# Six chunks of q, k and v requested at the start, decode steps spaced differently, and two memory layouts exchanged

## The chip, the cores and the metric

The kernel runs on one core of a Trainium2 chip. The metric is the device time of one execution in microseconds (us), as the median of several runs. The core has five engines with a queue of instructions each: TensorE (PE, matrix products), VectorE (DVE), ScalarE (ACT), GpSimd (POOL) and SyncE (SP). An engine works through its own queue in order: an instruction that waits holds up everything behind it on that engine. SP does nothing but issue transfers (through hardware descriptors, queue q1); POOL computes and also issues transfers (through software descriptors, queue q0).

## What is computed

Three stages, in fp32 accuracy: a decayed linear attention over 4 batches, 8 heads, 768 positions and 64 values a head; a gated product without a nonlinearity; and an FFN with a sigmoid-gated activation.

```
state = gamma * state + k[t]^T v[t];  y[t] = q[t] @ state / sqrt(64)     # x: 3072 x 512
h = (x @ w1) * (x @ w2) @ w3;  x = h @ w_out                             # 512 -> 1024 -> 512
h = x @ w_in;  out = (h * sigmoid(1.702 h)) @ w_out2                     # 512 -> 2048 -> 512
```

The weights arrive as 64-bit words and are turned into fp32 on the chip.

## The kernel before, in words

**Products.** Every fp32 operand of a large product is split into a rounded high part and a low remainder, and `mm3` (lines 240 to 242) issues three matmuls in place of one: high by high, weights high by operand low, weights low by operand high. The high part is made by a cast (`nc.scalar.copy` on ACT, in `split` or `upper`), the low part by a subtraction on DVE (`residue` or `lower`). So PE's second or third matmul of a group waits for DVE.

**Decoding weights.** `weight_steps` is a generator over 36 weight tiles (8 of w1 and w2, 4 of w_out, 8 of w3, 16 of the FFN). Each `yield` ends one step, which is one DVE instruction; a tile takes ten: two clamps (L184), two shifts (L192), two merges of the low word (L196), two sign merges (L205), and two subtractions for the low part (L137), which stand behind the clamps of the next tile. `magnitude` (L128) is the ACT instruction at the head of a tile; it reads `raw`, the buffer that a transfer on SP fills (`fetch`, L118). `work(n)` runs n steps, and so decides where in each engine's queue they stand.

**Attention (0 to about 155 us).** 24 chunks `c` of 128 tokens. For a chunk PE computes scores `s` (L339), the state update `u` (L365) and the output `y` (L389, L399); DVE masks the scores (`pt`, L351) and scales the output (`xb`, L411); ACT scales v (`vs`, L332) and copies the state. `load(c)` brings q, k, v of one chunk (1 MB) on POOL's queue into one of four buffers. `fill(c, at)` is called at four places `at` of a chunk and calls `work` there. From chunk 4 on, at the end of every second chunk, a gate follows (`first_gate`): 24 matmuls into `psg` with one decoded tile `wh`, `wl`; DVE multiplies its result into `h` (L279). Two chunks and a gate are called a period below.

**Mixed stage (155 to 417 us).** PE forms the gates of the other five blocks of 512 tokens and the product of w3 and w_out. POOL forms further operands (`st`, L159; `g`, L985 and L986) and stores them in DRAM (`sp`, `sw`, `sm`, `hd`). The last part takes its memory from pool `b2`.

**Blend (417 to 553 us).** A seven-product scheme for 2x2 blocks: 21 turns, `n` from 0 to 20, of 24 matmuls into `m`. In `blend`, turn n needs operand `l` (1 MB, loaded by SP from `hd`, L767, by `load_turn`), its cast `h` (ACT) and its remainder (DVE, L162). `todo(n)`, which is `ahead(n)`, does the remaining decode steps.

**FFN (553 to 1027 us).** `Expand` takes 4 blocks of 768 tokens by 8 weight tiles `left[j]`, in groups of 42 matmuls (`quad`) into banks `a`, `e`, `c`; a weight tile lies in one of eight slots (`slot`, table `SLOT`), is loaded from `sp` (`fetch_left`, L511) and split (`split_left`). `contract` is the last product, in 21 turns.

**Memory.** The pools of one stage lie on the addresses of the stage before. `reuse_waits="tile"` makes a new tile wait for the last user of each older tile that it overlaps, so the layout decides what a transfer waits for. In `b2` the tiles lie, in KiB from its start: `st` 0 to 8, `b12` 8 to 12, an unused gap 12 to 16, `g` 16 to 26 and 26 to 36. In the blend, on the same addresses, the operands `l` of turns 2, 3, 4 and 5 lie at 0 to 8, 24 to 32, 16 to 24 and 8 to 16.

Of the kernel before, what the change touches and what calls it, by code (L numbers as in the profile page):

```python
# [16 lines left out]
P = 128  # L17
NT = B * S
NCK = S // P
NC = B * NCK  # L20
# [22 lines left out]
def tile_kernel(  # L43
# [59 lines left out]

    fetched = used = 0
    allowed = R_BUFS

# [70 lines left out]
    def weight_steps():  # L177

        nonlocal used
        for i in range(len(tiles)):  # L180
            if i == 0:
                magnitude(i)
            for x in wx[i]:
# [19 lines left out]
            for n, (x, raw) in enumerate(zip(wx[i], raws[i])):  # L203
                bits = x.bitcast(I32)
                nc.vector.scalar_tensor_tensor(  # L205
                    bits, raw[:, :, 1], -(2**31), bits, ALU.bitwise_and, ALU.bitwise_or
                )
                if i < WI:
                    upper(i, n)
                used += 1  # L210
                fetch()
                fetch()
                magnitude(i + 1)
                if i >= WI and n:
                    seven(i, *wx[i])
                yield i + (i >= WI and n)
            if i < WI:
                lows[:] = [lambda i=i, n=n: lower(i, n) for n in range(2)]

    steps = weight_steps()  # L220
# [75 lines left out]
    class Attention:  # L296
# [21 lines left out]
        def load(self, c):  # L318
            t = self.tile("qkv", 2048, 4)
            for h in ((0, 1024), (1024, 2048)) if c == 0 else ((0, 2048),):  # L320
                nc.gpsimd.dma_start(t[:, slice(*h)], qkv[c][:, slice(*h)])
            qkt[c] = t[:, :1024].rearrange("p (a n t) -> p a n t", a=2, n=NP)
            kvt[c] = t[:, 1024:].rearrange("p (a h d) -> p a h d", a=2, h=H)

# [94 lines left out]
        def run(self, fill):  # L419

            self.scores(0)
            self.masked(0)
            for c in range(NC):
                if c + 1 < NC:
                    self.scores(c + 1)
                fill(c, 0)
                if c + 1 < NC:
                    self.masked(c + 1)
                fill(c, 1)
                self.updates(c)  # L430
                self.next_state(c)
                if c + 2 in range(2, NCK):
                    self.factors(c + 2)
                fill(c, 2)
                self.outputs(c)
                if c + 4 < NC:
                    self.load(c + 4)
                fill(c, 3)
# [59 lines left out]

    SLOT = "e", 0, 1, 2, 3, 4, 5, 6
    pools = {True: spare}  # L500
# [11 lines left out]

    def split_left(n):
        hi, lo = (left[n][:, w].rearrange("p b c -> p (b c)") for w in range(2))
        split(hi, lo, lo.bitcast(F32))

# [3 lines left out]
    class Expand:  # L520
# [75 lines left out]
        def run(self):  # L596
            self.open = nxt = None
            for n in range(1, NQ):
                left_tile(n)
                if n < NQ - 1:  # L600
                    fetch_left(n, nc.sync)
            self.results = [self.result(j) for j in range(2)]
            split_left(1)
            for s in range(NS):

                for j in range(NQ):

                    def step(at):
                        nonlocal nxt
                        more = s + 1 < NS  # L610
                        if more and (j, at) == (2, 3):
                            nxt = operands(s + 1, self.py)
                            next(nxt)
                        elif more and (j, at) in NEXT:
                            next(nxt)
# [7 lines left out]
            for _ in self.fourth():  # L623
                pass

    NEXT = (4, 3), (5, 1), (5, 3), (6, 3), (7, 0), (7, 2), (7, 3)
    RIGHT = dict(P1=0, P2=1, P3=2, P5=3, P6=4, P7=5, P4=6)
# [253 lines left out]
    with tc.manual_schedule():  # L881
# [4 lines left out]
        with (  # L886
            tc.tile_pool(name="p0", bufs=1, reuse_waits="tile") as p0,
            tc.tile_pool(name="ps0", bufs=1, space=PSUM, reuse_waits="tile") as ps0,
        ):
            attention = Attention(p0, ps0)  # L890
            nc.sync.dma_start(attention.dv, cv)
            nc.sync.dma_start(attention.mask, cmask)
            for c in range(4):
                attention.load(c)
# [14 lines left out]
            def fill(c, at):  # L909
                if (c, at) in ((0, 0), (1, 0)):  # L910
                    for _ in range(3 if c else 2):
                        fetch(held=True)
                if c > 1:
                    work(1 + (c > CPB and at == 2))
                while late:
# [14 lines left out]
        with (  # L930
# [43 lines left out]
            def gate_second(t, i, ab):  # L974
                nonlocal b12, g
                b = hb[0]
                if t % 2 == 0:
                    b12 = first_b.pop() if first_b else b12_tile()
                    g = pb.tile([P, 5, TB], F32, tag="g", bufs=2, name="g")
                    gate_out(b12, ab)  # L980
# [8 lines left out]

            g = None  # L990
            def b12_tile():
                return pb.tile([P, TB], F32, tag="b", bufs=2, name="b12")

            b12 = None
            for n, i in list(enumerate(ORDER))[1:]:
                nxt = ORDER[n + 1] if n + 1 < NB else None
                for t in range(KF):
# [16 lines left out]
                    while rows < KF and (complete > W3 + rows or (n, t) == (2, KF - 1)):  # L1014
# [4 lines left out]
                        if rows == KF:  # L1019
                            stage.close()  # L1020
                            pb = homes["st"] = stage.enter_context(
                                tc.tile_pool(name="b2", bufs=1, reuse_waits="tile")
                            )
                            st_ready = [pb.tile([P, 1024], F32, tag="st", bufs=2, name="st")]
                            first_b = [b12_tile()]
                            pb.tile([P, 1024], F32, name="gap")
        inner.close()
# [5 lines left out]
        def ahead(n):  # L1033
            nonlocal py, early
            if n == len(blends) - 2:
                split_left(0)
            if complete < len(tiles):
                work(4)
            elif n < 9:
# [125 lines left out]
```

## Time and profile before

| what | value |
|---|---|
| median of 3 runs | 1028.37 us (1027.59 to 1029.99) |
| the profiled execution | 1028.83 us; its span, from first to last instruction, 1027.1 us |
| busy share of the span: PE, DVE, ACT, POOL | 95%, 70%, 44%, 21% |
| mean granted clock of TensorE | 0.984 of full speed |
| moved by DMA | 268.73 MB, 262 GB/s on average |

The profile has one row for each instruction, with its start, its duration and the idle time of its engine ahead of it, with what ended that idle time in brackets. A busy share is an average over the stages; what a change is worth is read from the waits of the stage in which it acts. The granted clock has two levels here, 1.0 (2.4 GHz) and 0.5 (1.2 GHz); a value in between is a stretch with both.

### The profile page before, as it was taken

What the parts mean: (1) busy time and instruction counts of PE and PEld (TensorE: products, weight loads), DVE (VectorE), ACT (ScalarE), POOL (GpSimd) and SP (SyncE); (2) the same over time, 40 slices, a digit from 0 to 9 for tenths busy, and PEclk for the clock granted to TensorE, in tenths of its full rate; (3) what the DMA queues carried; (4) which work ended last, traced back from release to release, by engine and by line L of the source; (5) the groups of instructions that cost most, each with busy time, mean ns of one, the idle gap of its engine ahead of it and who ended that gap; (6) DMA issues with size and microseconds to landing.
All of it is one profiled execution on the core that took longest, in us unless ns stands there. A gap on an engine that the chain in (4) does not pass through costs nothing.

```text
span 1027.1 us, 14851 instructions
## 1 busy us (share of the span) xinstructions
PE 973.2 (95%) x5608; PEld 839.2 (82%) x5608; DVE 717.1 (70%) x959; ACT 449.7 (44%) x793; POOL 212.3 (21%) x248
## 2 busy tenths in 40 slices
PE   5899889999999999688998999999999999999998
PEld 5677768888888888567786999999999888888886
DVE  4766667888969867496774797685968555656662
ACT  4655564443322213263553664545455543445330
POOL 3010100048866745256202000000000000000000
PEclk9999999999999999889998999999999999999999
DMA  8778966568998979968956744646497978757871
GB/s 348 257 277 298 328 231 226 184 216 264 352 348 314 316 257 339 379 228 282 334 196 233 283 202 187 252 194 245 188 322 276 328 254 265 259 182 235 289 249 52
DMA packets 115032, 268.73 MB, mean 262 GB/s; under 512 B 7952, under 2 KB 69520, under 8 KB 105488
## 3 DMA queue, kind: packets, MB, share of 16 engines
q1 hardware_dynamic: 101264, 195.03, 54.2%
q0 software_dynamic: 13696, 72.75, 19.0%
q8 instruction: 44, 0.72, 0.3%
q14 instruction: 28, 0.23, 0.1%
HBM read 165.52 MB, written 102.24 MB: 261 GB/s over the span
## 4 chain that ended last, share of the span: by engine, by line
PE 48%; DMA 5%; POOL 4%; issue 3%; DVE 3%; ACT 1%; SPq 0%; POOLq 0%; DVEq 0%; ACTq 0%
PE m L241 9%; PE m L242 9%; PE m L240 9%; PE a L240 4%; PE a L242 4%; PE a L241 4%; PE e L242 2%; PE e L240 2%; PE e L241 2%; DMA hd<-g 2%; POOL st L159 1%; DMA raw<-in_wo_dram 1%; PE c L242 1%; PE c L240 1%; PE c L241 1%
## 5 line engine op out<-in xcount | busy, mean ns | idle before, releaser
L240 PE MATMUL psm<-xh,wh 128*128 128x512 f32 x320 | 124.6, 389 | 0.0
L242 PE MATMUL psm<-xh,wl 128*128 128x512 f32 x320 | 124.5, 389 | 0.0
L241 PE MATMUL psm<-xl,wh 128*128 128x512 f32 x320 | 124.5, 389 | 0.0
L240 PE MATMUL m<-h,op 128*128 128x512 f32 x320 | 124.5, 389 | 0.0
L242 PE MATMUL m<-h,op 128*128 128x512 f32 x320 | 124.5, 389 | 0.0
L241 PE MATMUL m<-l,op 128*128 128x512 f32 x304 | 118.3, 389 | 0.0
L662 ACT CAST h<-l 128x2048 fp32r<-128x2048 f32 x38 | 72.3, 1914 | 83.4 <-PE m L242 56.0
L663 DVE TENSOR_TENSOR l<-l,h 128x2048 fp32r<-128x2048 f32 x38 | 85.6, 2286 | 20.5 <-ACT h L662 20.5
L240 PE MATMUL a<-yh,op 128*128 128x384 f32 x256 | 86.2, 337 | 5.6 <-ACT s L531 5.1
L668 POOL DMA_DIRECT2D op<-sw x6 | 3.2, 531 | 400.5 <-PE a L242 220.1
L241 PE MATMUL a<-yl,op 128*128 128x384 f32 x256 | 85.9, 336 | 0.0
L242 PE MATMUL a<-yh,op 128*128 128x384 f32 x256 | 85.9, 336 | 0.0
L128 ACT ACTIVATE x<-raw 128x512 f32<-128x512 f32 x72 | 46.5, 675 | 75.2 <-DMA raw<-in_wo_dram 47.1
L240 PE MATMUL m<-h,wh 128*128 128x512 f32 x168 | 67.0, 399 | 9.5 <-ACT h L255 9.5
L240 PEld LDWEIGHTS psm<-xh,wh 128*128 128x128 f32 x320 | 60.1, 188 | 12.7 <-issue 0.2
L242 PEld LDWEIGHTS psm<-xh,wl 128*128 128x128 f32 x320 | 60.1, 188 | 12.5
L240 PEld LDWEIGHTS m<-h,op 128*128 128x128 f32 x320 | 60.1, 188 | 12.5
L242 PEld LDWEIGHTS m<-h,op 128*128 128x128 f32 x320 | 60.1, 188 | 12.3
L241 PEld LDWEIGHTS psm<-xl,wh 128*128 128x128 f32 x320 | 60.1, 188 | 12.3
L162 DVE TENSOR_TENSOR l<-l,h 128x2048 fp32r<-128x2048 f32 x19 | 46.4, 2441 | 33.2 <-ACT h L255 33.2
L242 PE MATMUL m<-h,wl 128*128 128x512 f32 x168 | 66.8, 398 | 0.0
L241 PEld LDWEIGHTS m<-l,op 128*128 128x128 f32 x304 | 57.1, 188 | 11.9
(149 smaller groups left out, 2228.2 us busy)
## 6 DMA issues: line engine op xcount, KB each, us to landing
gd<-g SPq DMA_DIRECT2D x32, 1344.0 KB, 4.7
qkv<-in_qkv_dram POOLq DMA_DIRECT2D x23, 1024.0 KB, 8.8
l<-gd SPq DMA_DIRECT2D x26, 768.0 KB, 6.7
l<-hd SPq DMA_DIRECT2D x19, 1024.0 KB, 6.9
raw<-in_w_dram SPq DMA_DIRECT2D x32, 512.0 KB, 5.5
hd<-g POOLq DMA_DIRECT2D x12, 1280.0 KB, 9.3
raw<-in_wo_dram SPq DMA_DIRECT2D x24, 512.0 KB, 8.3
l<-gd SPq DMA_DIRECT2D x24, 512.0 KB, 5.2
```

The source lines that it names most:

```text
L128: nc.scalar.activation(x, high, AF.Abs, scale=2.0**16)
L159: nc.gpsimd.tensor_tensor(out, x, y, op)
L162: nc.vector.tensor_tensor(lo, x, hi.bitcast(F32), ALU.subtract)
L240: nc.tensor.matmul(ps, wh, xh, start=start, stop=False, skip_group_check=True)
L241: nc.tensor.matmul(ps, wh, xl, start=False, stop=False, skip_group_check=True)
L242: nc.tensor.matmul(ps, wl, xh, start=False, stop=stop, skip_group_check=True)
L662: nc.scalar.copy(hi, x.bitcast(F32))
L663: nc.vector.tensor_tensor(x, x.bitcast(F32), hi.bitcast(F32), ALU.subtract)
L668: queue.dma_start(t.bitcast(F32), sw[PART[name]])
```

## The change

1. **Loads of q, k, v.** `load` is called for six chunks at the start instead of four. Chunks 4 and 5 take four buffers of the weight tiles (`wg`), which the last gate tiles need only later; the first half of chunk 0 is issued by SP ahead of its other transfers instead of by POOL. `load(c + 4)` starts at chunk 2. Three fetches of raw weights move from chunk 1 to chunk 2.
2. **Decode steps in the attention.** Tile 0's subtractions follow at once, and `fill` runs three steps more in chunks 4 and 5, so all later steps stand three places earlier.
3. **Pool `b2`.** The order of its tiles is `g` 0 to 10 and 10 to 20, `st` 20 to 28, `b12` 28 to 32 KiB.
4. **Decode steps in the blend.** `magnitude` is no longer issued right behind the fetch, but at the next call of `ahead`; and `ahead` runs two steps a turn instead of four up to turn 4.
5. **FFN.** The table `SLOT` gives tiles 1 to 7 the slots 1, 3, 4, 0, 2, 5, 6 instead of 0 to 6, and `left[1]` is cast by DVE instead of ACT. `NEXT0` moves two operand steps of the first block to later places.

```diff
@@ weight_steps
-            if i == 0:
-                magnitude(i)
+            magnitude(i)
...
-                magnitude(i + 1)
+                if not lazy:
+                    magnitude(i + 1)
...
+            if i == 0:
+                for k, f in enumerate(lows):
+                    f()
+                    yield k
+                lows.clear()
@@ Attention.load
-            t = self.tile("qkv", 2048, 4)
-            for h in ((0, 1024), (1024, 2048)) if c == 0 else ((0, 2048),):
-                nc.gpsimd.dma_start(t[:, slice(*h)], qkv[c][:, slice(*h)])
+            if c in (4, 5):
+                qk, kv = (
+                    homes["wg"].tile([P, 1024], F32, tag="wg", bufs=16, name=f"c{x}") for x in "qk"
+                )
+            else:
+                t = self.tile("qkv", 2048, 4)
+                qk, kv = t[:, :1024], t[:, 1024:]
+            if c in (0, 4, 5):
+                (nc.gpsimd if c else nc.sync).dma_start(qk, qkv[c][:, :1024])
+                nc.gpsimd.dma_start(kv, qkv[c][:, 1024:])
+            else:
+                nc.gpsimd.dma_start(t, qkv[c])
@@ Attention.run
-                if c + 4 < NC:
+                if 6 <= c + 4 < NC:
                     self.load(c + 4)
@@
-    SLOT = "e", 0, 1, 2, 3, 4, 5, 6
+    SLOT = "e", 1, 3, 4, 0, 2, 5, 6
@@ Expand.run
-            split_left(1)
+            split_left(1, nc.vector.tensor_copy)
...
+    NEXT0 = (4, 3), (6, 0), (6, 2), (6, 3), (7, 0), (7, 2), (7, 3)
@@
-            for c in range(4):
+            for c in range(1, 6):
                 attention.load(c)
@@ fill
-                if (c, at) in ((0, 0), (1, 0)):
+                if (c, at) in ((0, 0), (2, 0)):
                     for _ in range(3 if c else 2):
                         fetch(held=True)
                 if c > 1:
-                    work(1 + (c > CPB and at == 2))
+                    work(1 + (c >= CPB and at == 2) + (c in (CPB, CPB + 1) and at == 3))
@@ gate_second
-                    b12 = first_b.pop() if first_b else b12_tile()
-                    g = pb.tile([P, 5, TB], F32, tag="g", bufs=2, name="g")
+                    b12 = pb.tile([P, TB], F32, tag="b", bufs=2, name="b12")
+                    g = first_g.pop() if first_g else g_tile()
...
+                            first_g = [g_tile()]
                             st_ready = [pb.tile([P, 1024], F32, tag="st", bufs=2, name="st")]
-                            first_b = [b12_tile()]
-                            pb.tile([P, 1024], F32, name="gap")
@@ ahead
+            lazy = True
             if n == len(blends) - 2:
                 split_left(0)
             if complete < len(tiles):
-                work(4)
+                for i in sorted(raws):
+                    if i >= complete:
+                        magnitude(i)
+                work(2 if n < 5 else 4)
```

PE's instructions keep their order throughout. On DVE, in a period of the attention (from one gate's product `h` to the last row before the next one) the queue before reads:

```order
L279 TENSOR_TENSOR h<-h,psg 128x512
L351 TENSOR_TENSOR pt<-s,mask 128x512 x2
L192 TENSOR_SCALAR x<-x 128x512
L196 SCALAR_TENSOR_TENSOR x<-raw,x 128x512 x2
L411 TENSOR_TENSOR xb<-y,dy 128x512
L205 SCALAR_TENSOR_TENSOR x<-raw,x 128x512 x2
L351 TENSOR_TENSOR pt<-s,mask 128x512 x2
L184 TENSOR_SCALAR x<-x 128x512 x2
L137 TENSOR_TENSOR wl<-x,wh 128x512
L411 TENSOR_TENSOR xb<-y,dy 128x512
L137 TENSOR_TENSOR wl<-x,wh 128x512
L192 TENSOR_SCALAR x<-x 128x512
```

and after the change:

```order
L285 TENSOR_TENSOR h<-h,psg 128x512
L366 TENSOR_TENSOR pt<-s,mask 128x512 x2
L205 SCALAR_TENSOR_TENSOR x<-raw,x 128x512 x2
L184 TENSOR_SCALAR x<-x 128x512
L426 TENSOR_TENSOR xb<-y,dy 128x512
L184 TENSOR_SCALAR x<-x 128x512
L138 TENSOR_TENSOR wl<-x,wh 128x512
L366 TENSOR_TENSOR pt<-s,mask 128x512 x2
L138 TENSOR_TENSOR wl<-x,wh 128x512
L192 TENSOR_SCALAR x<-x 128x512 x2
L426 TENSOR_TENSOR xb<-y,dy 128x512
L196 SCALAR_TENSOR_TENSOR x<-raw,x 128x512 x2
```

The same twelve rows stand there; the two subtractions `wl`, which stood on either side of the period's last `xb`, now both stand ahead of it, the first one ahead of the second `pt`. On ACT, at the start of the blend, the queue before reads (casts `h` of turn 1 and of weights, then the rows of turns 0 and 1):

```order
L255 CAST wh<-wl 128x1024
L128 ACTIVATE x<-raw 128x512 x2
L821 COPY s<-m 128x512 x2
L255 CAST h<-l 128x2048
L255 CAST wh<-wl 128x1024
```

and after the change:

```order
L261 CAST wh<-wl 128x1024
L129 ACTIVATE x<-raw 128x512
L838 COPY s<-m 128x512 x2
L261 CAST h<-l 128x2048
L261 CAST wh<-wl 128x1024
```

One of the two reads of `raw` has left the place ahead of turn 2's cast `h`; it now stands behind turn 3's. On SP the loads around that place stand, before and then after:

```order
L767 DMA l<-hd_77 128x4x512 x2
L118 DMA raw<-in_wo_dram 128x1024
L767 DMA l<-hd_77 128x4x512
L118 DMA raw<-in_wo_dram 128x1024
L767 DMA l<-hd_77 128x4x512
```

```order
L784 DMA l<-hd_77 128x4x512 x3
L119 DMA raw<-in_wo_dram 128x1024
L784 DMA l<-hd_77 128x4x512
L119 DMA raw<-in_wo_dram 128x1024
L784 DMA l<-hd_77 128x4x512
```

The first `raw` moved behind a third load of `l`.

## Rows read from the trace of the kernel before

**Rows 1.** Waits of PE, whole span: total us, times, longest.

```profile
PE psg L242 <- DVE wl L137: 14.0, 8, 3.6
PE m L240 <- ACT h L255: 9.5, 1, 9.5
...
PE m L241 <- DVE l L162: 5.7, 4, 3.0
PE a L240 <- ACT s L531: 5.1, 1, 5.1
PE s L339 <- DVE pt L351: 2.8, 1, 2.8
```

**Rows 2.** Busy time by stretch: PE, PEld, DVE, ACT, POOL, PE clock, DMA share, GB/s.

```profile
24.53:30.00 5.47, 5.47 (x74) 4.83 (x76) 4.79 (x10) 3.62 (x12) 0.06 (x1) 0.69 0.84 346
54.95:68.51 13.56, 12.31 (x153) 9.78 (x152) 9.32 (x17) 7.38 (x23) 1.33 (x2) 1.00 0.84 300
133.00:139.81 6.81, 6.81 (x23) 5.18 (x23) 2.07 (x4) 1.86 (x7) 0.00 (x0) 0.75 0.68 259
438.65:445.50 6.85, 5.32 (x13) 3.86 (x14) 6.85 (x7) 5.75 (x7) 2.67 (x4) 0.54 0.58 226
...
560.31:567.00 6.69, 6.69 (x28) 6.69 (x29) 3.90 (x3) 2.88 (x4) 0.00 (x0) 0.69 1.02 425
```

**Rows 3.** Timeline of PE: a gate's first matmul; turn 2's first matmul.

```profile
61.31 0.50 PE L240 MATMUL psg<-xh,wh 128*128 128x512 f32 x1
...
438.65 0.80 PE L240 MATMUL m<-h,wh 128*128 128x512 f32 x1 [9.49 <-ACT h L255]
```

**Rows 4.** Timeline of DVE: start, duration, idle before.

```profile
22.14 1.74 DVE L184 TENSOR_SCALAR x<-x 128x512 f32<-128x512 f32 x1 [1.17 <-ACT x L128]
...
58.89 0.68 DVE L411 TENSOR_TENSOR xb<-y,dy 128x512 f32<-128x512 f32 x1
...
60.69 1.28 DVE L351 TENSOR_TENSOR pt<-s,mask 128x512 f32<-128x512 f32 x2
61.89 0.75 DVE L184 TENSOR_SCALAR x<-x 128x512 f32<-128x512 f32 x2
62.56 0.68 DVE L137 TENSOR_TENSOR wl<-x,wh 128x512 fp32r<-128x512 f32 x1
...
464.17 4.52 DVE L162 TENSOR_TENSOR l<-l,h 128x2048 fp32r<-128x2048 f32 x1
...
525.11 0.55 DVE L467 CAST yh<-yr 128x768 fp32r<-128x768 f32 x1
```

**Rows 5.** Timeline of POOL at the start: five loads of q, k, v.

```profile
1.28 2.76 POOL L321 DMA_DIRECT2D qkv<-in_qkv_dram  x5 [0.37 <-issue]
```

**Rows 6.** Timeline of SP at the start of the blend.

```profile
406.10 23.12 SPq L767 DMA_DIRECT2D l<-hd  x2
429.33 0.55 SPq L118 DMA_DIRECT2D raw<-in_wo_dram  x1
```

**Rows 7.** DMA issues in 60:150, 413:415, 428.6:429: count, KB, us to landing.

```profile
raw<-in_w_dram SPq DMA_DIRECT2D x7, 512.0 KB, 10.1
...
hd<-g POOLq DMA_DIRECT2D x1, 1280.0 KB, 8.8
...
l<-hd SPq DMA_DIRECT2D x1, 1024.0 KB, 5.2
```

**Rows 8.** Timeline of ACT: a blend's raw read, turn 18's copy, the FFN's cast.

```profile
435.18 0.66 ACT L128 ACTIVATE x<-raw 128x512 f32<-128x512 f32 x1 [15.17 <-DMA raw<-in_wo_dram]
...
542.23 0.59 ACT L821 COPY s<-m 128x512 f32<-128x512 f32 x1 [2.13 <-PE m L242]
...
558.20 1.68 ACT L255 CAST op<-op 128x1792 fp32r<-128x1792 f32 x1 [4.50 <-DMA op<-sp]
```

**Rows 9.** Timeline of POOL: the last two stores of `g`.

```profile
413.67 0.57 POOL L987 DMA_DIRECT2D hd<-g  x1 [0.30 <-POOL g L986]
...
421.59 0.57 POOL L987 DMA_DIRECT2D hd<-g  x1 [0.30 <-POOL g L986]
```

More of the change, by code (lines that the diff above doesn't have):

```diff
@@ L104, in tile_kernel @@
     fetched = used = 0
+    lazy = False
     allowed = R_BUFS
@@ L318, in load @@
         def load(self, c):
-            t = self.tile("qkv", 2048, 4)
-            for h in ((0, 1024), (1024, 2048)) if c == 0 else ((0, 2048),):
-                nc.gpsimd.dma_start(t[:, slice(*h)], qkv[c][:, slice(*h)])
-            qkt[c] = t[:, :1024].rearrange("p (a n t) -> p a n t", a=2, n=NP)
-            kvt[c] = t[:, 1024:].rearrange("p (a h d) -> p a h d", a=2, h=H)
+            if c in (4, 5):
[10 more added lines that the diff above has]
+                nc.gpsimd.dma_start(t, qkv[c])
+            qkt[c] = qk.rearrange("p (a n t) -> p a n t", a=2, n=NP)
+            kvt[c] = kv.rearrange("p (a h d) -> p a h d", a=2, h=H)
         def bank(self, kind):
@@ L511, in fetch_left, with split_left @@
         queue.dma_start(t.bitcast(F32), sp[n])
-    def split_left(n):
+    def split_left(n, copy=nc.scalar.copy):
         hi, lo = (left[n][:, w].rearrange("p b c -> p (b c)") for w in range(2))
-        split(hi, lo, lo.bitcast(F32))
+        copy(hi, lo.bitcast(F32))
+        residue(hi, lo, lo.bitcast(F32))
     def left_parts(n, name, k):
@@ L597, in run @@
             self.open = nxt = None
-            for n in range(1, NQ):
+            for n in sorted(range(1, NQ), key=lambda n: SLOT[n]):
                 left_tile(n)
-                if n < NQ - 1:
-                    fetch_left(n, nc.sync)
+            for n in range(1, NQ - 1):
+                fetch_left(n, nc.sync)
             self.results = [self.result(j) for j in range(2)]
-            split_left(1)
+            split_left(1, nc.vector.tensor_copy)
             for s in range(NS):
@@ L613, in step @@
                             next(nxt)
-                        elif more and (j, at) in NEXT:
+                        elif more and (j, at) in (NEXT if s else NEXT0):
                             next(nxt)
@@ L890, in tile_kernel @@
             attention = Attention(p0, ps0)
+            attention.load(0)
             nc.sync.dma_start(attention.dv, cv)
             nc.sync.dma_start(attention.mask, cmask)
-            for c in range(4):
+            for c in range(1, 6):
                 attention.load(c)
@@ L988, in gate_second, with g_tile @@
                 hb.pop(0)
[L990 to L994, printed above, removed]
+            def g_tile():
+                return pb.tile([P, 5, TB], F32, tag="g", bufs=2, name="g")
+            b12 = g = None
             for n, i in list(enumerate(ORDER))[1:]:
@@ L1033, in ahead @@
         def ahead(n):
-            nonlocal py, early
+            nonlocal py, early, lazy
+            lazy = True
             if n == len(blends) - 2:
```

## The prediction

> **What bounds the kernel now.** PE is busy 95% of the span, and its instructions keep their order and number; the change can only take away idle time of PE, and time in which PE runs at the lower clock. I read the waits of PE first [rows 1]: five of them hold 37 us, in three places. Eight gates of the attention wait 14.0 us for `wl`; one turn of the blend waits 9.5 us for a cast `h`, and four wait 5.7 us for a remainder `l`; the FFN's first group waits 5.1 us for a copy on ACT; chunk 2 waits 2.8 us for a mask. Then the busy time by stretch [rows 2]: behind the long waits PE is busy throughout, yet at a granted clock between 0.54 and 0.75, so each long wait costs a second time. Last the timelines, for what is late at each place.
>
> **The gates.** In a period DVE starts `xb` at 58.89 and, after two sign merges, the second mask at 60.69; the gate's first matmul runs at 61.31, but DVE comes to the first `wl` only at 62.56, behind mask and clamps [rows 3, 4]. That is the wait: on average (14.0 - 3.6) / 7 = 1.5 us, and 3.6 once. After the change three instructions of the same forms stand between the first mask and `xb` (two merges and a clamp instead of two merges and a shift), so `xb` keeps its place. Behind it stand one clamp (0.75 / 2 = 0.38) and the first `wl` (0.68): 58.89 + 0.68 + 0.38 + 0.68 = 60.6, ahead of the gate's start by 0.7. The mask (1.28) and the second `wl` (0.68) end at 62.6; the second half of the gate needs it from 64.2 on (the gate lasts 68.51 - 61.31 - 1.5 = 5.7). What now stands behind, two shifts and two merges, is wanted by nobody before the next period. The period shrinks from 13.56 to 12.06; DVE is busy 9.32 of it, ACT 7.38 [rows 2], so neither becomes the bound. I take all 14.0; at most 15.5, since PE's modelled matmul ends shorten the idle time that a row shows. The longest wait is followed by 6.81 us at clock 0.75 [rows 2]: (1 - 0.75) x 6.81 = 1.7 us, gone with it. Sum 15.7.
>
> **The start.** In chunk 2 a clamp on DVE takes 1.74 us instead of 0.38 [rows 4]; a multiplication by POOL runs at the same moment, because a load stands ahead of it in POOL's queue and waits for a buffer. After the change no load stands between the first four multiplications, so they are done earlier, and the mask behind the clamp comes 1.4 earlier: the wait of 2.8 halves. The 5.47 us behind it ran at 0.69 [rows 2], which is 1.7 us; the 1.4 us that stay are no longer than the gates' waits, beside which the clock stays at 1.00 (54.95 to 68.51 in [rows 2]), so I take all 1.7. Bounds for both: 0 (the raw weights are later now, and the wait stays) and 4.5. SP's first load takes one issue out of POOL's queue, 2.76 / 5 = 0.55 [rows 5]: I take 0.5, bounds 0 and 0.55. Sum 3.6.
>
> **The blend.** Now SP stands for 23 us at the load of turn 3's `l` [rows 6], whose memory (24 to 32 KiB) overlaps both buffers of `g`; the last store of `g` is issued at 421.59 [rows 9], and the load leaves about 428.7 (the row ends at 429.2, and one issue takes 0.55). The raw weights behind it are issued at 429.33 [rows 6], and ACT, which reads them ahead of turn 2's cast, stands 15.17 us until 435.18 [rows 8]. PE is free for turn 2 at 438.65 - 9.49 = 429.16 [rows 3]. After the change that read stands behind turn 3's cast. But turn 2's own load now overlaps the first buffer of `g` (0 to 10 KiB), so it waits for the store issued at 413.67, which landed 8.8 us later, at 422.5 [rows 7, 9]; before, it waited for none of these. That store shared the engines with turn 2's load, which is now behind it, so it lands somewhat sooner: 421 to 422.5, I take 421.5. A load of `l` takes 5.2 us alone and a transfer beside others 8.8 [rows 7]; the last store of `g` runs beside it, I take 6.5. Landing 428.0; the cast takes 1.9 (1.68 for 1792 columns [rows 8], so for 2048): 429.9, a wait of 0.7 instead of 9.5, so 8.8 gained; bounds 9.5 (landing 426) and 5.5 (landing 431.3, a wait of 4.0). With so short a wait the 5.32 busy us at clock 0.54 [rows 2] go too: 2.4 us, bounds 0 and 2.4. Turn 4's load now waits for the last `g` and lands about 434 to 437, while its turn starts at about 441: hidden, with 3 us of cover after the cast. The remainders: 5.7 us [rows 1], of which 3.0 where DVE needed 4.52 us for one beside POOL's work [rows 4]. DVE does two steps a turn less, some 1.3 us; but in turn 2 the remainder still follows the cast and PE waits about 2 for it, and POOL's work meets DVE at other turns. I leave 3.5 of the 5.7: 2.2 gained, bounds 0 and 3.5. Sum 13.4, bounds 5.5 and 15.4.
>
> **The FFN.** ACT stands 4.50 us until `left[1]` has landed and casts it for 1.68 [rows 8], with the first group's copies behind it. Slot 0, where it lay, overlaps by the sizes the weights of the blend's last turn; slot 1 overlaps those of turn 18 and earlier, and turn 18 ends at 542.2 [rows 8]. The load therefore starts two turns earlier and lands by 551 even at 8.8 us. Its cast is on DVE now: 0.55 for 768 columns [rows 4], an estimated 1.3 for 1792, and a remainder of 1792 / 512 x 0.68 = 2.4; done by 555, while the second group, which needs it, starts some 6 us after 553 (36 matmuls of 384 columns against 24 of 512 in 5.7). ACT goes on to the copies at once. The wait of 5.1 goes, and with it (1 - 0.69) x 6.69 = 2.1 at the lower clock [rows 1, 2]. Sum 7.2, bounds 2 (DVE late instead of ACT) and 7.2.
>
> **Sum.** 15.7 + 3.6 + 13.4 + 7.2 = 39.9. The mixed stage is not touched but for addresses; PE is busy there without a gap. From this I take off 0.9 for transfers that come late in the shorter attention: in a period DMA has a share of 0.84 and moves 300 GB/s x 13.56 us = 4.07 MB [rows 2]; in 12.06 us the share is 0.94, and in the two periods in which four reloads of 256 KB run, 1.06, that is up to 1.5 us too much in all. The Trainium skill ("DMA: Bandwidth & Descriptors", Specifications) puts a core's limit at HBM at about 358 GB/s; by it the reload periods need 12.8 us and 1.5 us are lost. The FFN's start moved 425 GB/s [rows 2], above that figure; at that rate nothing is lost. So 39.0: the profiled execution, 1028.83, becomes 989.8. It lies 0.5 above the median shown; as a median 989.4.
>
> **Rivals.** (a) DMA becomes the bound of the attention: raw weights or reloads come late in each period from chunk 13 on, and up to four gates wait 1.5 us again. For it the share of 0.94; against it that q, k, v are asked six chunks ahead. 1.5 to 6 us back: 991 to 996. (b) Turn 2's load is late: at the upper bounds the wait is 4.0, the clock falls again (1.5), the remainders gain nothing (2.2): 7 back, 996. For it that 1 MB now starts at 421.5 and not at 406.10 [rows 6]; against it that the raw weights no longer stand in the way. (c) `left[1]` is late and DVE stands for it: 5 back, 995. (d) The gates wait as before, because DVE reaches `xb` late and everything behind it with it: 14 back, 1003; against it DVE's idle 4.2 us in the period. (e) Slower than before: POOL's queue, which now always holds further loads, starves SP's raw weights, and ACT stands at their read ahead of the casts of each tile. They land 10.1 us after their issue [rows 7] and are asked two periods, 24 us, ahead; each us beyond that costs PE one per tile. To eat 39 us, eight tiles must lose 5 us each: it decides from a landing time of 29 us, three times the row; then 1029 or more. The Trainium skill (same page, Queues, rings and completion order) says that a DMA engine takes turns between the queues that have work for it; by that rule SP's loads get their turn however long POOL's list is. No row here has six loads asked ahead. (f) The waits only change their place, and the time stays within 0.2%.
>
> **Chances.** Forecast as summed 0.56 (985 to 993); (a) 0.12; (b) 0.16; (c) 0.05; (d) 0.04; two of these together, 996 to 1004, 0.02; (e) 0.03; (f) 0.02. So faster by more than 0.2% (what a measurement of this kernel can tell from no change) 0.95, within it 0.02, slower 0.03. The range runs from all upper bounds together (15.5 + 1.7, 5.05, 15.4, 7.2: 44.9, so 983) to 1001, which takes in (a), (b) and (c) and leaves out less than 2 in 10. The likeliest case's own range is 985 to 993.
>
> **What the profile will show.** Right: no wait of `psg` for `wl` above 0.3 us, and a period of about 12; a mean clock above 0.99; turn 2's cast no later than 1 us after PE is free for it; ACT's read of `raw` behind turn 3's cast, with no wait of PE behind it; `left[1]` loaded at the end of turn 18, and no idle PE at the FFN's start. Wrong: a wait of PE for q, k, v or of ACT for `raw` in the attention (a, e); `l` of turn 2 landing after 430 (b); a long remainder beside POOL's `st` in turns 5 to 7; DVE idle ahead of its cast of `left[1]` (c). It would be wrong as a whole if PE, freed of these waits, met a wait that they hid, for instance for `xb` in the attention.

## The result, and the profile after

The changed kernel takes 1011.59 us (median of 4 runs, 1010.01 to 1012.48) against 1028.78 of the kernel before on the same chip: a ratio of 0.9831, interval 0.9813 to 0.9849. It is faster, as forecast, but by 17 us where 39 were forecast, and it lies outside the range of 983 to 1001. Its profiled execution has a span of 1009.2 us at a mean granted clock of 0.986.

Where the 17.9 us between the two profiled executions (1028.83 and 1010.95) came from is seen in the starts of the stages on PE (the first matmul into `psg`, `psm`, `m` and `a` in its timeline). The forecasts of the start and the gates are given in one sum, with the 0.9 for late transfers taken off:

| stage | before | after | gained | forecast |
|---|---|---|---|---|
| up to the second gate | 47.32 | 50.88 | -3.6 | } 18.4 |
| second gate to the mixed stage | 108.1 | 92.8 | 15.3 | } |
| mixed stage | 261.3 | 261.3 | 0 | 0 |
| blend | 136.1 | 132.7 | 3.4 | 13.4 |
| first stage of the FFN | 241.0 | 238.4 | 2.6 | 7.2 |

PE's waits after, which answer to [rows 1]:

```profile
PE s L354 <- DMA qkv<-in_qkv_dram: 9.4, 3, 4.4
PE m L247 <- DVE l L163: 5.6, 4, 1.8
PE m L246 <- ACT h L261: 4.9, 2, 3.2
PE a L246 <- ACT s L547: 2.9, 1, 2.9
PE psg L246 <- ACT xh L261: 2.9, 1, 2.9
...
PE s L354 <- DVE pt L366: 1.7, 1, 1.7
...
PE psg L248 <- DVE wl L138: 0.4, 1, 0.4
```

The 14.0 us for `wl` are gone. The 9.5 us for one cast `h` are now 4.9 us for two; the 5.7 us for remainders are 5.6, at other turns; the 5.1 us for a copy at the FFN's start are 2.9; and 2.9 us for `xh` are new, ahead of the first gate. The first line, the waits of the first chunks for q, k and v, was 8.3 us before: the first load now comes 1.2 us earlier, but that of chunk 1 comes later, and PE starts chunk 1 0.75 us later than before (before, then after):

```profile
10.14 2.08 PE L339 MATMUL s<-qkv 64*128 64x128 f32 x16 [2.46 <-DMA qkv<-in_qkv_dram]
```

```profile
10.89 2.08 PE L354 MATMUL s<-qkv 64*128 64x128 f32 x16 [4.41 <-DMA qkv<-in_qkv_dram]
```

Busy time by stretch, with the columns of [rows 2]: the start, the first gate, a period, turn 2, turn 7, the FFN's start.

```profile
20.00:30.00 10.00, 8.29 (x128) 7.02 (x127) 6.96 (x17) 6.65 (x22) 2.14 (x4) 0.83 1.03 417
30.00:35.96 5.96, 2.40 (x50) 1.83 (x49) 1.30 (x4) 2.35 (x4) 0.08 (x1) 0.92 1.01 414
35.96:44.92 8.96, 8.55 (x25) 5.98 (x25) 6.22 (x12) 6.42 (x21) 0.00 (x0) 0.67 0.44 158
56.57:68.62 12.05, 12.05 (x154) 9.86 (x153) 9.32 (x17) 7.20 (x23) 1.67 (x2) 1.00 0.87 312
420.49:430.40 9.91, 8.17 (x25) 6.19 (x25) 9.00 (x8) 5.86 (x7) 0.84 (x1) 0.66 1.03 388
454.36:464.34 9.98, 8.16 (x24) 6.29 (x25) 7.89 (x9) 3.30 (x4) 3.69 (x7) 0.66 0.78 274
542.92:549.60 6.68, 6.68 (x29) 6.68 (x30) 2.77 (x3) 2.88 (x4) 0.00 (x0) 0.74 0.89 367
```

The period is 12.05 us, where 12.06 was forecast, and PE is busy all of it. But behind each new wait PE runs at a clock of 0.66 to 0.74, as behind the old ones: a turn that takes 5.44 us undisturbed takes 9.9. PE's rows at the new waits, and ACT's, which shows what was late:

```profile
35.96 0.79 PE L246 MATMUL psg<-xh,wh 128*128 128x512 f32 x1 [2.94 <-ACT xh L261]
...
420.49 0.64 PE L246 MATMUL m<-h,wh 128*128 128x512 f32 x1 [3.16 <-ACT h L261]
...
454.36 0.50 PE L246 MATMUL m<-h,wh 128*128 128x512 f32 x1 [1.73 <-ACT h L261]
...
542.92 0.45 PE L246 MATMUL a<-yh,op 128*128 128x384 f32 x1 [2.95 <-ACT s L547]
```

```profile
34.22 0.66 ACT L129 ACTIVATE x<-raw 128x512 f32<-128x512 f32 x1 [3.09 <-DMA raw<-in_w_dram]
...
418.54 1.90 ACT L261 CAST h<-l 128x2048 fp32r<-128x2048 f32 x1 [5.97 <-DMA l<-hd]
...
451.86 0.66 ACT L129 ACTIVATE x<-raw 128x512 f32<-128x512 f32 x1 [7.99 <-DMA raw<-in_wo_dram]
452.42 1.89 ACT L261 CAST h<-l 128x2048 fp32r<-128x2048 f32 x1
...
542.39 0.48 ACT L547 COPY s<-a 128x384 f32<-128x384 f32 x1 [3.90 <-DMA yd<-s]
```

All four are ACT standing for a transfer: a raw weight ahead of the cast `xh` that the first gate needs; the load of `l` of turn 2; a raw weight ahead of turn 7's cast; and, at the FFN, a *store*, since the first copy `s` lies where a buffer of the blend lay that is still being written to `yd`. How long these transfers took (the median where there are two), from the DMA issues of 21:22, 409.8:410.6, 441.5:442.3 and 534:538 (count, KB, us to landing):

```profile
raw<-in_w_dram SPq DMA_DIRECT2D x2, 512.0 KB, 10.8
...
l<-hd SPq DMA_DIRECT2D x1, 1024.0 KB, 8.5
...
raw<-in_wo_dram SPq DMA_DIRECT2D x1, 512.0 KB, 9.9
...
yd<-s POOLq DMA_DIRECT2D x2, 256.0 KB, 6.8
```

Of the two raws in the first line, the one that ACT stands for took 12.4 us. Between 20 and 36 us DMA moves 414 to 417 GB/s without a gap. That is again above the limit of about 358 GB/s that the Trainium skill ("DMA: Bandwidth & Descriptors", Specifications) gives for a core at HBM; here the trace decides.

### The profile page after: what moved, and what is told of

It reads as the page before. It is cut to its first block, busy times and chain, and to the rows that moved or that the text cites. A ratio compares the mean times of both kernels' runs of the same rounds, so it can differ in the third digit from the quotient of the medians.

```text
span 1009.2 us, 14859 instructions
## 1 busy us (share of the span) xinstructions
PE 973.4 (96%) x5608; PEld 840.3 (83%) x5608; DVE 716.2 (71%) x960; ACT 447.4 (44%) x792; POOL 205.2 (20%) x249
## 3 DMA queue, kind: packets, MB, share of 16 engines
q0 software_dynamic: 13840, 72.23, 18.4%
## 4 chain that ended last, share of the span: by engine, by line
PE 47%; DVE 2%; DMA 1%; issue 0%; ACT 0%; POOL 0%; DVEq 0%; ACTq 0%
PE m L247 9%; PE m L248 9%; PE m L246 9%; PE a L247 4%; PE a L246 4%; PE a L248 4%; PE e L248 2%; PE e L247 2%; PE e L246 2%; PE c L248 1%; PE c L247 1%; PE c L246 1%; DMA yd<-s 1%; DVE g L579 1%; DVE yl L483 0%
## 5 line engine op out<-in xcount | busy, mean ns | idle before, releaser
L680 DVE TENSOR_TENSOR l<-l,h 128x2048 fp32r<-128x2048 f32 x38 | 85.6, 2287 | 20.3 <-ACT h L679 20.3
L248 PEld LDWEIGHTS psm<-xh,wl 128*128 128x128 f32 x320 | 60.1, 188 | 12.4
L247 PE MATMUL m<-l,wh 128*128 128x512 f32 x152 | 61.7, 406 | 5.6 <-DVE l L163 5.6
```

The lines of the kernel that those rows point to most:

```text
L247: nc.tensor.matmul(ps, wh, xl, start=False, stop=False, skip_group_check=True)
L248: nc.tensor.matmul(ps, wl, xh, start=False, stop=stop, skip_group_check=True)
L680: nc.vector.tensor_tensor(x, x.bitcast(F32), hi.bitcast(F32), ALU.subtract)
```

## The experiments

All start from the changed kernel, and every one was timed beside the kernel before. Stage starts and lengths are read as in the table above; "turns 1 to 3" is the sum of three turns, 16.3 us undisturbed. A turn is measured from its first matmul to the next turn's, so a wait ahead of a turn's first matmul counts to the turn before. The times were taken in four sittings, one of them on another chip, in which the kernel before took 1028.8 to 1030.7 us; between sittings the ratios compare better than the medians.

| kernel | median us | ratio to before, interval | first gate | mixed stage | blend | FFN, first stage |
|---|---|---|---|---|---|---|
| changed | 1011.59 | 0.9831, 0.9813 to 0.9849 | 35.96 | 143.66 | 132.7 | 238.4 |
| four chunks | 1003.33 | 0.9759, 0.9727 to 0.9791 | 32.77 | 138.47 | 130.3 | 237.3 |
| raws in chunk 1 | 1002.72 | 0.9736, 0.9712 to 0.9759 | 33.60 | 138.29 | 130.5 | 238.8 |
| b2 mended | 1006.10 | 0.9775, 0.9753 to 0.9797 | 36.18 | 145.64 | 125.5 | 238.6 |
| raw read later | 1012.20 | 0.9827, 0.9799 to 0.9855 | 36.20 | 145.26 | 133.0 | 238.6 |
| last raw early | 1009.31 | 0.9783, 0.9764 to 0.9803 | 35.65 | 143.78 | 130.7 | 239.0 |
| copies on the last store | 1015.99 | 0.9861, 0.9847 to 0.9876 | 36.27 | 145.17 | 130.7 | 243.2 |
| old blend pacing | 1018.01 | 0.9865, 0.9843 to 0.9888 | 36.44 | 146.69 | 137.6 | 239.8 |
| four mends | 1004.67 | 0.9747, 0.9732 to 0.9762 | 33.00 | 138.10 | 125.4 | 244.1 |
| copies clear | 1005.58 | 0.9772, 0.9746 to 0.9798 | 35.68 | 144.03 | 128.7 | 234.0 |
| old slots | 1010.61 | 0.9830, 0.9801 to 0.9860 | 34.82 | 143.13 | 132.4 | 237.9 |
| old b2 | 1010.18 | 0.9809, 0.9786 to 0.9833 | 35.80 | 147.44 | 127.7 | 240.0 |
| five mends | 992.51 | 0.9650, 0.9617 to 0.9682 | 32.92 | 138.28 | 121.7 | 234.8 |

The stages come from one profile of each kernel, and single profiles differ. Five kernels of this table leave the code of the blend as the changed kernel has it (four chunks, raws in chunk 1, copies on the last store, copies clear, old slots), and their blend takes 128.7 to 132.4 us; the changed kernel's 132.7 is the longest of the six. Turn 2's wait for `h` is 3.1 to 3.2 us in all six; turn 7's goes from 0.4 to 3.0, and those of turns 12 and 13 differ too.

### The start: four chunks, or the raw fetches in chunk 1

The first kernel takes the old `load`, its old calls and the old place of the fetches; the second only the last of these edits:

```diff
...
-            attention.load(0)
...
-            for c in range(1, 6):
+            for c in range(4):
                 attention.load(c)
...
-                if (c, at) in ((0, 0), (2, 0)):
+                if (c, at) in ((0, 0), (1, 0)):
```

> The start is that of the kernel before (four chunks asked at once, all by POOL; three raw fetches in chunk 1); all other parts stay as changed. Theory S: the start lost time because the longer list keeps DMA full until 36 us and the first raw weights land 11 to 14 us after their issue. Then the first gate starts at about 33 us instead of 35.96, behind no wait for xh, and its period is 12.05 instead of 14.9: the mixed stage starts at about 138 instead of 143.66, the time falls by 5 to 6, to about 1006. Rival P: the new pacing itself (tile 0's subtractions at once, three steps more in chunks 4 and 5) makes the first gate late: it stays at about 36 and the time at 1011.6. Rival Q: the two further chunks pay later: periods behind the first gate become longer than 12.1 and the time is not better than 1011.

> Only the three fetches of raw weights go back from chunk 2 to chunk 1; six chunks are still asked at the start. Theory S, if the lateness is that of the issue: the raws are asked some 4 us earlier, ACT's wait of 3.1 us at their read is gone, the first gate starts at 33 to 34 and runs at the full clock: 2 to 5 us gained, 1007 to 1010. Rival: DMA has no room until 36 us (410 GB/s in all slices), so the raws only take the place of chunks: the first gate starts no earlier than 35.5, or a wait for a chunk takes its place, and the time stays within 1 us of 1011.6.

Both bring the first gate back to 33 us and the mixed stage to 138.3, 5.2 and 5.4 us earlier, so the pacing is not at fault (rival P falls) and the two further chunks pay nothing that the stage shows. The second kernel tells cause from company: six chunks are asked and DMA is as full as ever (419 GB/s in 20:33), yet the raws, asked from 18.8 us on instead of 21.3 and landing 9.7 us later, are there when ACT comes to them, and the first gate runs at full clock:

```profile
29.34 1.23 ACT L129 ACTIVATE x<-raw 128x512 f32<-128x512 f32 x2
```

```profile
33.60:42.50 8.90, 8.67 (x78) 6.61 (x74) 7.46 (x15) 6.32 (x21) 0.00 (x0) 1.00 0.63 253
```

So it is the later request of three raws into a full DMA that cost the start, not the longer list by itself. The raw that ACT stands for is asked 2.6 us later in the changed kernel and lands 5.2 us later (12.4 us after its request instead of 9.7): two loads of 1 MB, which were asked behind the raws, are now asked ahead of them. Whether the later request would cost as much with four chunks, no run shows.

The kernel with four chunks differs in the FFN too: there the loads of `left` start only with the FFN, at 530.2 us, the copies wait for no store, and DVE is 1.4 us late with `left[1]`. Why these loads move is not shown; what follows from it is tried further below.

### The blend: layout, read of raw, last raw, pacing

> Pool b2 is laid out as st 0 to 8, last g 8 to 18, last but one g 18 to 28, b12 28 to 32 KiB, so that turn 2's load of l overlaps no g, turn 3's only the last but one, and turn 5's the last. Theory B: turn 2's loss (3.16 wait for h, 1.74 for l, 2.7 at the lower clock) is the landing of its load behind a store of g, and goes: 7 to 7.6 us, the FFN starts at about 530.3 instead of 537.7, time about 1004. Rival: the raws behind the loads now land elsewhere, ACT stands at one of them ahead of another turn's cast, or turn 3's load is late in place of turn 2's: a gain under 3 us, with a wait of h at turn 3 or 4.

```diff
+            gs = [0]
             def g_tile():
-                return pb.tile([P, 5, TB], F32, tag="g", bufs=2, name="g")
+                gs[0] += 1
+                return pb.tile([P, 5, TB], F32, tag=f"g{gs[0] % 2}", name="g")
...
-                            first_g = [g_tile()]
                             st_ready = [pb.tile([P, 1024], F32, tag="st", bufs=2, name="st")]
+                            first_g = [g_tile(), g_tile()]
+                            gs[0] = 1
```

The blend is 7.2 us shorter, the amount that theory B gives, but only part of it by theory B's cause. Turn 2's cast has no wait left, and turn 3's costs PE 0.63:

```profile
414.47 1.92 ACT L261 CAST h<-l 128x2048 fp32r<-128x2048 f32 x1
...
423.44 1.91 ACT L261 CAST h<-l 128x2048 fp32r<-128x2048 f32 x1 [3.48 <-DMA l<-hd]
```

Turns 1 to 3 gain 4.7 (19.4 us, where the six kernels above take 23.6 to 24.5): this is the layout's. Turns 6 and 7 gain 2.3 and turn 12 1.4, about as much as they differ by among those six (15.5 to 18.3 and 5.4 to 7.2), and turns 4 and 5 lose 1.0.

> In the blend ACT's read of raw is issued one call of ahead later than in the changed kernel, so that it stands behind the cast of the next turn. Theory R: turn 7's loss (1.73 and 0.47 for h, 1.82 for l, 2.7 at the lower clock) is ACT standing 8 us at a raw that landed 10 us after its issue, ahead of turn 7's cast: it goes, 6 to 6.7 us, time about 1005. Rival: DVE, which works in order, then waits for x ahead of the remainders, and the waits change from h to l: a gain under 2 us, or a loss.

```diff
...
-                for i in sorted(raws):
+                for i in due:
                     if i >= complete:
                         magnitude(i)
+                due = sorted(raws)
```

A miss, and neither theory's: turn 7 waits 2.6 and 1.5. The read that ACT stands at there, 8.87 us at 454.59, had not moved, since it is not issued by this loop but by the decode step itself, which begins a tile with `magnitude(i)`. What is late is the request: the last half tile is fetched by a decode step of turn 5, and in SP's queue it stands behind the load of turn 8, which waits for the end of turn 4:

```profile
430.36 11.40 SPq L784 DMA_DIRECT2D l<-hd  x3
441.86 0.57 SPq L119 DMA_DIRECT2D raw<-in_wo_dram  x1
```

(changed kernel). The next run asks for it earlier:

> The changed kernel, but in the blend up to five fetches of raw weights may be open instead of three, so that the last half tile is asked two turns earlier, ahead of the loads of turns 5 to 8 in SP's queue and not behind the load of turn 8. Theory R, as it stands after the reading of raw was moved without effect: turn 7's loss (0.47 and 1.73 for h, 1.82 for l, 2.7 at the lower clock) is the late request of that raw, for which ACT stands 8 us ahead of turn 7's cast. Then it goes: 6 to 6.7 us, time about 1005. Rival: with DMA at a share of 0.95 there the earlier raw makes a load of l late (turns 3 to 5), or ACT stands at it there: a gain under 2 us, or none.

```diff
...
             lazy = True
+            allowed = R_BUFS
```

Turns 6 and 7 fall from 17.6 to 11.5 us, 6.2 less, and no read of raw is waited for there: theory R holds. But the blend as a whole falls by 2.0 only, since the wait at turn 12 grows: DVE stands for `yr`, which the blend loads for the FFN, ahead of turn 12's remainder, and that turn takes 11.8 us instead of 7.2.

```profile
478.72 0.96 DVE L487 TENSOR_TENSOR yt<-yr 128x768 f32<-128x768 f32 x1 [4.27 <-DMA yr<-yd]
```

> The changed kernel with the blend's decode steps as before: four a turn, and the read of raw issued right behind its fetch. Theory R: the last raw is fetched at turn 4 at the latest, so turn 7's loss goes; the read of raw ahead of turn 3's cast costs little, since that raw lands at 427.3 and turn 3 starts at 430.4: a gain of 4 to 6, time 1006 to 1008, and the new pacing would be no part of the gain. Rival: reads of raw ahead of the casts of turns 3 to 5 cost as much as turn 7 does now, and DVE's steps beside POOL's work give back remainders of 3 us as in the kernel before: 1011 or more.

```diff
-            lazy = True
...
-                for i in sorted(raws):
-                    if i >= complete:
-                        magnitude(i)
-                work(2 if n < 5 else 4)
+                work(4)
```

The rival holds, and more than that: ACT stands 16.8 us at a read of raw ahead of turn 2's cast, as before the change [rows 8], and PE 10.9 us.

```profile
427.86 0.66 ACT L129 ACTIVATE x<-raw 128x512 f32<-128x512 f32 x1 [16.80 <-DMA raw<-in_wo_dram]
```

> The changed kernel with pool b2 laid out as before, the new decode pacing kept. Theory B: turn 2's load waits for no store and turn 2 starts without a wait; turn 3's load waits for the last g and lands about 425, so turn 3 waits some 3 for its cast, about 1.8 for the remainder and 2.5 at the lower clock: turns 1 to 3 take about as long as in the changed kernel, blend 129 to 133. Rival: a read of raw stands ahead of turn 2's cast again, as with the old pacing (10.9 us there): blend 137 or more.

```diff
...
-                            first_g = [g_tile()]
                             st_ready = [pb.tile([P, 1024], F32, tag="st", bufs=2, name="st")]
+                            first_b = [b12_tile()]
+                            pb.tile([P, 1024], F32, name="gap")
```

`b2` has its old order (`st`, `b12`, gap, `g`) again. Turn 2 starts without a wait, as theory B has it, but turn 3 waits 1.5 us and not 3, and the blend is 127.7, shorter than the 129 to 133 expected. Turns 1 to 3 take 21.9 us, 2.3 less than in the changed kernel and 1.8 to 2.7 less than in the six profiles with the new layout; turns 12 and 13 take 2.0 less, which is within their spread. With the blends of before (136.1: both old, but with the other parts of the change old too) and of the last run (137.6: old pacing, new layout) there is one profile for each of the four cases: the pacing is worth 5 to 8 us in either layout, and the new layout gains nothing in either; in turns 1 to 3 it costs 1.4 with the old pacing and 2.3 with the new. The total of this profile hides it: its attention ends 3.8 us later than the changed kernel's (the last chunk waits 2.6 us for its load, 0.6 there), and its FFN takes 1.6 more.

### The FFN: where the first copies lie

> The changed kernel, but one unused tile is taken first in the FFN's pool, so that its first copies s lie where no store of the blend's last turns reads. Theory F: the wait of 2.95 at the FFN's start is ACT's wait for a store of yd that landed 7 us after its issue beside the early loads of left; without the overlap it goes, and 2.1 at the lower clock behind it: the first stage of the FFN takes 233.4 instead of 238.4, time about 1006.5. Rival: the next thing is late there, left[1]'s remainder on DVE or left[2] on ACT (a wait of 1.44 for DVE stood there in the kernel with four chunks): under 2 us gained.

```diff
+            self.p.tile([P, TS], F32, tag="s", bufs=6, name="skip")
             self.results = [self.result(j) for j in range(2)]
```

A miss by its edit, and useful: the unused tile pulled the whole group of copies to the front of the pool, onto the buffer of the blend's last store. The wait followed that store, from 2.95 to 7.3 us:

```profile
546.22 0.48 ACT L547 COPY s<-a 128x384 f32<-128x384 f32 x1 [8.23 <-DMA yd<-c]
```

> The changed kernel, but the FFN's copies s lie between its two result tiles, where their first tile overlaps no buffer that a late store of yd reads (in the run before, the tile had moved onto the very last store, and the wait grew from 2.95 to 7.3). Theory F: now the wait at the FFN's start goes, and the 2.1 at the lower clock with it: the first stage of the FFN takes 233.4 to 235 instead of 238.4, time about 1007. Rival: left[1]'s remainder on DVE or left[2]'s load is late at the same place: under 2 us gained.

```diff
-            self.results = [self.result(j) for j in range(2)]
+            self.results = [self.result(0)]
+            self.p.tile([P, TS], F32, tag="s", bufs=6, name="skip")
+            self.results.append(self.result(1))
```

Theory F holds: PE meets no wait at the FFN's start, the first stage takes 234.0, 4.4 less, and the kernel 1005.6. What the kernel gains beyond the 4.4 is no effect of this edit: the blend, which it leaves alone, took 4.1 less in this profile, within its spread.

> The changed kernel with the slots of the kernel before; left[1] is still cast by DVE. Theory F says that the early loads of left make the stores of yd late: with the old slots the loads start at the FFN's start, the last stores land 2 to 3 us after their issue as before, ACT's first copies go at once, and what is late is left[1] on DVE by about 1.4 us, as in the kernel with four chunks, where the loads also started late: first stage 237.3 instead of 238.4, so 1 us faster than with the new slots. Rival: the stores are late whatever the loads do: the wait for s stays at 3 and the wait for left[1] comes on top: 241 or more.

```diff
-    SLOT = "e", 1, 3, 4, 0, 2, 5, 6
+    SLOT = "e", 0, 1, 2, 3, 4, 5, 6
```

As theory F has it. The loads now start at the FFN's start, the last stores land in 2.5 us instead of 6.8, the copies go at once, and DVE is late with `left[1]` (DMA issues of 533:536.5, and PE's waits):

```profile
yd<-s POOLq DMA_DIRECT2D x2, 256.0 KB, 2.5
```

```profile
PE a L248 <- DVE op L163: 1.4, 1, 1.4
```

The first stage takes 237.9, half a microsecond less than with the new slots: the early loads took from the stores what they gave to `left[1]`. With the old slots the stage is still 3.2 shorter than before, so the new slots have no part in the FFN's gain as the change stands; that leaves the cast on DVE, and the moved operand steps of `NEXT0`, which no run takes back.

### All together

> The changed kernel with four mends together: raw fetches in chunk 1, b2 as in the layout run, the last raw early, the FFN's first copies beside no store. If the four losses are what the missing part of the forecast is made of, and do not depend on each other: 5.4 (start) + 7.2 (turn 2) + 4.5 (what turns 6 and 7 lose in the layout run) + 5.1 (FFN) = 22 less than 1011.6, so 989 to 991; the blend takes about 121, the FFN starts at about 520. Rival: the gains overlap, since an earlier stage only hands its transfers on to the next wait: 995 to 1001.

The start comes out as summed (138.1). The blend takes 125.4 where 121 was expected, with a wait at turn 12 (that turn takes 9.3 us), and the FFN's edit was that of the run with the copies on the last store, which costs 5.7 there against the changed kernel. With that edit corrected, and the operand steps one turn later:

> The four mends, with the FFN's copies laid clear as in the first run of this set, and the operand steps of the FFN one turn later in the blend (a wait of 1.9 us and 1.9 at the lower clock stood at turn 12 with four mends, where DVE stands 2.9 us for yr ahead of the remainder l). Expected: mixed stage from 138.1, blend 121.5 instead of 125.4, first stage of the FFN 233.4 to 235 instead of 244: 988 to 991. Rival: the waits move on once more (turn 13, or the FFN's first operands, which are now made later): 993 to 1000.

```diff
...
-            else:
+            elif n > 10:
                 next(early, None)
```

992.51 us (989.27 to 995.78); the profiled run, 990.92, lies in the expected 988 to 991, the median 1.5 above it; two of the four runs lie in the rival's 993 to 1000. It is faster than both kernels. PE's waits:

```profile
PE s L354 <- DMA qkv<-in_qkv_dram: 9.7, 3, 4.4
...
PE m L247 <- DVE l L163: 2.3, 2, 1.9
...
PE m L246 <- ACT h L261: 1.0, 1, 1.0
PE a L246 <- ACT u L547: 0.9, 1, 0.9
PE psg L248 <- DVE wl L138: 0.2, 1, 0.2
```

The mean granted clock is 0.998. The span, 989.2, is 20.0 below that of the changed kernel; the forecast missed by 21.2 against its profile.

## Why the prediction was wrong, step by step

**The gates (15.7): right.** The waits for `wl` fell from 14.0 to 0.4 us, and the clock that was lost behind the longest of them came back. From the second gate on 15.3 us were gained, and with the raws in time the first gate's wait goes too: 17.4 from the first gate to the mixed stage (122.1 before, 104.7 in the second run), which is near the upper bound of 15.5 + 1.7. That DVE's order is the cause is read from its queue; no run takes the order back alone. The loads are not the cause: with the old ones 16.4 of the 17.4 stand.

**The start (3.6): wrong in sign, -3.6.** The step that failed is the bound of 0, "the raw weights are later now, and the wait stays", which did not look further than chunk 2: the raws made the first gate start 2.9 us late, behind a wait for `xh`, and run at clock 0.67, so that its period took 14.9 us and not 12.1. Up to this wait the kernel was 0.3 us ahead of the kernel before (PE is free at 33.02, before at 33.33). The landing time that the text had was that of periods in which DMA had room, 10.1 us, for a request 24 us ahead; at the start the request is 9 us ahead and the raw takes 12.4. Rival (e) named the mechanism, ACT at a raw ahead of a cast, but priced it only as a permanent one. Its idea that POOL's long list starves SP's queue is not borne out as a cause by itself: in the second run the same list stands, and the raws are in time.

Two smaller terms of the start went otherwise too. SP's first load was to gain 0.5; the first load did come 1.2 earlier, but chunk 1 started 0.75 later. And the wait for the mask shrank as forecast, 2.8 to 1.7, but "no longer than the gates' waits ... I take all 1.7" did not hold in this profile: the clock in 24:30 was 0.72, as before. It can go the other way. Of the nine kernels with this same start, four show 0.72 there after a mask wait of 1.6 to 1.7 us, and five, after one of 1.6, show 1.00. For example the changed kernel, then b2 mended:

```profile
24.00:30.00 6.00, 5.85 (x78) 5.11 (x78) 5.32 (x12) 2.79 (x10) 0.45 (x1) 0.72 1.02 417
```

```profile
24.00:30.00 6.00, 4.62 (x76) 3.83 (x77) 5.31 (x11) 2.87 (x11) 0.53 (x1) 1.00 1.02 415
```

**The blend (13.4, came 3.4): three sizes wrong.** In the five other kernels with the same blend the gain would have been 3.7 to 7.5, so the miss is 6 to 10 us. (1) The wait of turn 2: 3.16 instead of 0.7. The store landed as reckoned and the load left at 409.95, that is 421.7 on the old scale, 11.8 later, where 421.5 was forecast; but it took 8.5 us and not 6.5, with the last store of `g`, the loads of turns 3 and 4 and a load of `left` beside it. This is rival (b), short of its bound of 4.0. (2) "With so short a wait the 5.32 busy us at clock 0.54 go too: 2.4 us". None of it went: turn 2 lost 2.5 us beyond its waits after waits of 9.49 and 1.53, and 2.7 after 3.16 and 1.74. (3) The remainders: 2.2 forecast; nothing came in this profile, 0.7 to 2.0 in the five others.

To these comes a loss that the text has no term for: the last raw, which stood behind the load of turn 5 in SP's queue, stands behind that of turn 8 with the new pacing, and makes turn 7 wait for its cast and its remainder. The text followed SP's queue only to turn 4. Turn 12 waits 1.4 us more, where DVE stands 2.39 us for `yr` instead of 0.80; `yr` is asked in turn 9 in both kernels and lands 11.3 us after its request instead of 8.7. Why is open, and among the six profiles this wait comes and goes.

**The FFN (7.2, came 2.6): a wait behind the one removed.** The loads did start two turns earlier and `left[1]` was split in time. The step that failed is "ACT goes on to the copies at once": the copies lie on a buffer of the blend's, and its store lands late because of the very loads that were moved forward. The text followed what the new slots overlap, and not what the first copies overlap.

**The clock, throughout.** 7.9 us of the 39 (1.7, 1.7, 2.4, 2.1) were clock that was to come back with shorter waits. It came back where the waits went, at the gates and in the run with five mends (0.998). Where a wait was only made shorter it came back in some profiles and not in others.

**The chances.** The terms missed in three stages at once, for which the text left 0.02 (two of its rivals together). Two of the three causes, the first gate's raws and the store under the FFN's copies, were not among its rivals as priced.

## What to carry to other kernels

When a transfer is moved, ask what else is in flight at its new place, and what the next stage's first tiles lie on: raws asked 4 us later than before met a full DMA, turn 2's load met the stores of `g`, the FFN's early weights delayed stores whose buffers its first copies needed, and each of these waits stood on ACT, which feeds PE. Follow the queue of the engine that waits past the place of the change, to the last item that the new pacing moves. And take the clock's gain as certain only for waits that vanish.

## What the runs showed of the hardware

- The granted clock after a wait does not follow from the wait's length alone. Turn 2 lost 2.5 us beyond its waits after 9.49 and 1.53 us, and 2.7 after 3.16 and 1.74. Nearly equal waits went both ways: turn 7 with b2 mended (1.07 us for `h`, 1.82 for `l`) ran at 1.00 throughout, turn 3 with five mends (1.01 and 1.89) at 0.82, and took 1.7 us longer:

```profile
452.78:460.45 7.67, 5.85 (x25) 4.61 (x26) 7.67 (x9) 3.30 (x4) 2.44 (x5) 1.00 0.97 311
```

```profile
418.43:427.81 9.38, 7.49 (x24) 5.75 (x25) 6.86 (x6) 6.53 (x8) 4.95 (x7) 0.82 0.98 369
```

- At the FFN's start, against the 234.0 of a first stage without a wait, waits of 5.13 and 0.49 cost 1.4 beyond themselves, one of 2.95 cost 1.5.
- A store of 256 KB that landed in 2.4 to 2.5 us with no load of `left` beside it took 6.8 with two loads of 896 KB in flight and three more asked before it landed.
- Turn 7's wait for `h`, which hangs on one landing, differed from 0.4 to 3.0 us among kernels with the same decode pacing, and the attention's last chunk came 0.4 to 2.6 us late: a few microseconds between single profiles are no effect of an edit.
